# A depthwise-separable layer on one core: the first chunk of x and the third part of pw change places in the load queues

## The chip, the core and the metric

The kernel runs on one core of a Trainium2 chip. The core has a matrix engine (TensorE, PE in the profile; its weight loads are PEld), VectorE (DVE), ScalarE (ACT), GpSimd (POOL) and SyncE (SP), which here only issues transfers. Transfers between the chip's main memory (HBM) and the on-chip memory run on 16 DMA engines that all queues share. The metric is the device time of one launch in microseconds (us), the median of several runs.

## The reference

x has 384 x 384 pixels of 384 channels in bf16; dw holds one factor per channel; pw is a 384 x 384 matrix.

```python
H = W = 384
C = 384
k = 1
"x": normal(1, H, W, C) * 0.05,  "dw": normal(k, k, C) * 0.05,  "pw": normal(C, C) * 0.05

out = out + xp[:, i:i+H, j:j+W, :] * dw[i, j][None, None, None, :]   # one i, one j
return jnp.einsum('bhwc,cd->bhwd', out, pw)
```

With a 1 x 1 kernel this is one matrix product for each of 147,456 pixels: out = x · (dw ∘ pw), where row c of pw is scaled by dw[c].

## The kernel before

The factor dw is folded into pw once, at the start; after that the kernel is a stream of matrix products. Work is cut into 288 supertiles of 512 pixels. Supertiles are grouped into chunks, one load and mostly one store each: the first chunks hold 1, 1, 1, 1, 2 and 4 supertiles, the long middle 10 each, and the last ones 1 again.

**The early loads (lines 117 to 129).** `load_early` (its DMA stands at line 118 in the profile) issues five loads before anything else: dw on ScalarE's queue, three parts of pw with 128 rows each (96 KB; k = 0, 1, 2), and the first chunk of x (`X0_e`, 128 rows of 3072 bytes, 384 KB). Each load has a semaphore of its own: `s_dw`, `s_pw[0..2]`, `s_x[0][0]`. The parts k = 0 and 1 of pw and then the chunk of x are on SyncE's queue; the part k = 2 is on ScalarE's, behind dw. Each engine issues in program order. After these, SyncE goes on to its own list (`load_x`, line 170 in the profile, and `store`, line 210), sorted by due time: x's second chunk comes first. ScalarE goes on with a copy that warms it up (line 371) and then its copies below. The profile calls SyncE's queue q1 and ScalarE's q10.

**The fold (lines 278 to 314, 411 to 444).** TensorE starts with matmuls on constants that nobody reads (`idle_work`, line 134), which keep it busy until data comes. Three tiny matmuls at line 282 turn dw from a row into a column. VectorE multiplies a selection matrix by it (line 429; one call for each half of part 0, one for part 1, one for part 2). Then TensorE multiplies the selection matrix with pw, at line 306, in six units (k, r), r = 0, 1: the units of part k wait for `s_pw[k]` at line 297 as well as for VectorE's scaled selection at line 295, and part 2 also waits for the first copy out, since it writes the same PSUM banks. Unit (2, 0) runs its pair of matmuls twice. The list `w_units` (line 212) says who copies which unit from PSUM to `w_r` (line 416): VectorE the second half of unit 1 and the whole of unit 2, ScalarE the rest.

**The product (lines 252 to 275, 315 to 319).** For each supertile VectorE transposes x in 32 x 32 blocks (line 398 for the three first pieces of the first supertile, line 400 for everything else). TensorE then runs 48 matmuls at line 264, in 12 groups of four that use 32 rows of the array each and run side by side. Its first one waits for the copies of units 0 to 3 and for the first transpose; later steps of the first supertile wait for units 4 and 5. ScalarE copies each result from PSUM to the output buffer (line 469), and SyncE stores it.

The order on VectorE around the start is: scaled selections, its two copies of line 416, the transposes of the first supertile (which wait for `s_x[0][0]`), those of the second (which wait for x's second chunk). On TensorE it is: idle work, line 282, idle work, line 306 for part 0, 1 and 2, line 264.

Of the kernel before, what the change touches and what calls it, by code (L numbers as in the profile page):

```python
# [27 lines left out]
def kernel(  # L28
# [12 lines left out]
    nc = tc.nc  # L41
    P = nc.NUM_PARTITIONS
# [53 lines left out]
    s_x = [[nc.alloc_semaphore(f"s_x{i}{k}") for k in range(max(map(len, groups[i::NR])))] for i in range(NR)]  # L96
# [10 lines left out]
    s_pw = [nc.alloc_semaphore(f"s_pw{k}") for k in range(3)]  # L107
# [9 lines left out]
    def load_early(eng, dst, src, sem):  # L117
        ins = eng.dma_start(dst, src).then_inc(sem, 16)
        tc.no_tile_sem_insts.add(ins.ins.name)
        early.append(ins.ins.name)  # L120

    dw_e = dataclasses.replace(dw_h, donated_from="early_dw").ap()
    pw_e = [dataclasses.replace(raw_h, donated_from=f"early_pw{k}").ap()[:, D * k : D * k + D] for k in range(3)]
    load_early(nc.scalar, dw_e, dw.rearrange("a e c -> a (e c)"), s_dw)
    for k in range(3):
        load_early(nc.scalar if k == 2 else nc.sync, pw_e[k], pw[P * k : P * k + P, :], s_pw[k])
    x0 = xf[0:512, :].rearrange("(p s) c -> p (s c)", p=P)
    X0_e = dataclasses.replace(X0_h, donated_from="early_x0").ap()[:, 0:4].rearrange("p s c -> p (s c)")
    load_early(nc.sync, X0_e, x0, s_x[0][0])

    def idle_work(ps, n):
        for _ in range(n):
# [382 lines left out]
```

## Time and profile before

| what | us |
|---|---|
| median of 3 runs | 573.72 |
| lowest and highest run | 573.1, 574.96 |
| the profiled execution's own time | 573.13 |
| its span, first to last instruction | 571.2 |

All times within the profile count from the start of the span. A group of the profile gives a line, an engine, an operation, what it writes and reads, the count, the busy time and the mean time of one; what stands behind "idle before" is the engine's idle time ahead of the group and the event that ended most of it. A row of the timeline has start, length, engine, line and operation. A row of the DMA issues ends with the time from the issue to the last byte's landing. A row of the stretches has from:to, the length, then busy time and count of each engine, the granted clock, the DMA engines' share and GB/s.

### The profile page before, as it was taken

What the parts mean: (1) busy time and instruction counts of PE and PEld (TensorE: products, weight loads), DVE (VectorE), ACT (ScalarE), POOL (GpSimd) and SP (SyncE); (2) the same over time, 40 slices, a digit from 0 to 9 for tenths busy, and PEclk for the clock granted to TensorE, in tenths of its full rate; (3) what the DMA queues carried; (4) which work ended last, traced back from release to release, by engine and by line L of the source; (5) the groups of instructions that cost most, each with busy time, mean ns of one, the idle gap of its engine ahead of it and who ended that gap; (6) DMA issues with size and microseconds to landing.
All of it is one profiled execution on the core that took longest, in us unless ns stands there. A gap on an engine that the chain in (4) does not pass through costs nothing.

```text
span 571.2 us, 29717 instructions
## 1 busy us (share of the span) xinstructions
PE 566.9 (99%) x13841; PEld 364.2 (64%) x13841; DVE 509.3 (89%) x591; ACT 418.4 (73%) x297; POOL 13.9 (2%) x41
## 2 busy tenths in 40 slices
PE   9999999999999999999999999999999999999997
PEld 4666666666666666666666666666666666666664
DVE  7899999999999999999999999999999999999996
ACT  6777777777777777777777777777777777777775
POOL 2051000000000000000000000000000000000000
PEclk9999999999999999999999999999999999999999
DMA  8999999999999999999999999999999999997777
GB/s 323 447 385 394 432 420 428 440 421 417 425 430 430 411 379 423 411 384 392 428 399 389 413 428 400 399 410 426 399 379 425 402 392 404 417 392 317 321 286 270
DMA packets 28100, 226.88 MB, mean 397 GB/s; under 512 B 1465, under 2 KB 7866, under 8 KB 24122
## 3 DMA queue, kind: packets, MB, share of 16 engines
q1 hardware_dynamic: 27012, 225.81, 97.6%
q10 hardware_dynamic: 1078, 0.98, 0.5%
q14 instruction: 9, 0.07, 0.0%
q8 instruction: 1, 0.02, 0.0%
HBM read 113.54 MB, written 113.25 MB: 397 GB/s over the span
## 4 chain that ended last, share of the span: by engine, by line
PE 99%; ACT 0%; issue 0%
PE ps L264 98%; PE ps L306 0%; PE ps L134 0%; PE ps L341 0%; PE ps L329 0%; ACT O L464 0%; PE ps L282 0%
## 5 line engine op out<-in xcount | busy, mean ns | idle before, releaser
L264 PE MATMUL ps<-w_r,T 32*128 32x384 bf16 x13776 | 560.1, 321 | 0.0
L400 DVE STREAM_TRANSPOSE T<-X 128x384 uint32<-128x384 uint32 x571 | 500.7, 878 | 54.3 <-DMA X<-in_x_dram 1.1
L469 ACT CAST O<-ps 128x1536 bf16<-128x1536 f32 x286 | 411.7, 1440 | 146.7 <-PE ps L264 146.7
L264 PEld LDWEIGHTS ps<-w_r,T 32*128 32x128 bf16 x13776 | 361.6, 93 | 198.9 <-DVE T L398 0.7
L370 POOL COPY Xk<-Xl 32x256 bf16<-32x256 bf16 x16 | 6.3, 394 | 0.0
L369 POOL COPY Xk<-Xl 32x128 bf16<-32x128 bf16 x16 | 4.6, 288 | 25.2 <-DMA Xl<-in_x_dram 24.4
L416 ACT CAST w_r<-ps 128x768 bf16<-128x768 f32 (+1 forms) x5 | 3.4, 741 | 0.2 <-PE ps L306 0.2
L364 POOL COPY raw<-w_r 32x768 bf16<-32x768 bf16 x4 | 3.3, 820 | 5.9 <-ACT w_r L416 5.7
L134 PE MATMUL ps<-const-bfloat16-1.0 32*128 32x384 bf16 x24 | 2.2, 512 | 0.8 <-PEq L499 0.8
L371 ACT ACT_TABLE_LOAD x1 | 1.3, 1283 | 1.9 <-issue 1.9
L306 PE MATMUL ps<-raw 64*128 64x384 bf16 x14 | 2.6, 510 | 0.1
L460 DVE CAST O<-ps 128x384 bf16<-128x384 f32 x2 | 1.0, 553 | 1.4 <-PE ps L264 1.4
L306 PEld LDWEIGHTS ps<-raw 64*128 64x128 bf16 x14 | 0.8, 108 | 1.9 <-DVE raw L429 1.3
L400 DVE STREAM_TRANSPOSE T<-Xl 128x384 uint32<-128x384 uint32 x2 | 1.8, 880 | 0.2
L416 DVE CAST w_r<-ps 128x384 bf16<-128x384 f32 (+1 forms) x2 | 1.5, 758 | 0.3 <-PE ps L306 0.3
L383 DVE STREAM_TRANSPOSE T<-Xk 128x384 uint32<-128x384 uint32 x2 | 1.2, 578 | 0.5 <-PE ps L264 0.4
L341 PE MATMUL ps<-raw,T 128*128 128x384 bf16 x8 | 1.5, 327 | 0.0
L464 ACT CAST O<-ps 128x384 bf16<-128x384 f32 x2 | 1.0, 479 | 0.7 <-PE ps L341 0.7
L464 DVE CAST O<-ps 128x384 bf16<-128x384 f32 x2 | 1.1, 558 | 0.1
L459 ACT CAST O<-ps 128x384 bf16<-128x384 f32 x2 | 0.9, 482 | 0.5 <-PE ps L264 0.5
L341 PEld LDWEIGHTS ps<-raw,T 128*128 128x128 bf16 x8 | 0.7, 98 | 0.7 <-issue 0.3
L429 DVE TENSOR_SCALAR raw<-sel,ps 128x128 bf16<-128x128 f32 x2 | 0.5, 288 | 0.6 <-PE ps L282 0.6
(17 smaller groups left out, 5.0 us busy)
## 6 DMA issues: line engine op xcount, KB each, us to landing
X<-in_x_dram SPq DMA_DIRECT2D x25, 3840.0 KB, 21.8
out_dram<-O SPq DMA_DIRECT2D x25, 3840.0 KB, 27.7
X<-in_x_dram SPq DMA_DIRECT2D x3, 1536.0 KB, 18.6
X<-in_x_dram SPq DMA_DIRECT2D x2, 1920.0 KB, 14.5
out_dram<-O SPq DMA_DIRECT2D x2, 1920.0 KB, 24.0
out_dram<-O SPq DMA_DIRECT2D x2, 1536.0 KB, 13.1
X<-in_x_dram SPq DMA_DIRECT2D x6, 384.0 KB, 5.5
out_dram<-O SPq DMA_DIRECT2D x3, 768.0 KB, 5.9
```

Source lines behind the costliest of these rows:

```text
L134: mm = nc.tensor.matmul(ps[:, 2 * (i % 2) + i // 2, :D], lhsT=ones[32 * i : 32 * i + 32, 0:P], rhs=ones[32 * i : 32 * i + 32, :], start=Tr ...
L264: mm = nc.tensor.matmul(PS[s][:, q, :D], lhsT=Ts[s][32 * q : 32 * q + 32, b, par::2], rhs=w_r[32 * q : 32 * q + 32, b, par, :], start=(b, ...
L306: mm = nc.tensor.matmul(PS[(k + 1) % 2][:, 2 * r + v, :D], lhsT=sel_w[64 * v : 64 * v + 64, k, r, :, :].rearrange("p q w -> p (q w)"), rhs ...
L341: mm = nc.tensor.matmul(PS[1][:, m, :D], lhsT=Tk[:, P * (m + 2) : P * (m + 3), par], rhs=w_k[:, par, :], start=False, stop=par == 1,)
L364: nc.gpsimd.tensor_copy(w_k[quads[n]], w_r[quads[n], n]).then_inc(s_wk)
L369: nc.gpsimd.tensor_copy(Xk[quads[n], g:8:4, :], x_b).then_inc(s_xk)
L370: nc.gpsimd.tensor_copy(Xk[quads[n], 8 + g : 24 : 4, :], Xl[quads[g], :, 64 * n : 64 * n + 64]).then_inc(s_xk)
L371: nc.scalar.copy(warm[:, 0:1], nc.const_aps.tensor(0.0, [P, 1], F32)).then_inc(s_a[0])
L400: ins = nc.vector.transpose(out=Tw[:, 3 * h : 3 * h + 3], in_=Xw[:, :, j, 96 * h : 96 * h + 96].rearrange("p k (b w) -> p b k w", w=32),)
L416: o = nc.vector.tensor_copy(out, in_) if e == 0 else nc.scalar.copy(out, in_)
L464: o = (nc.scalar.copy if n % 2 else nc.vector.tensor_copy)(Ov[:, n, j, :], PS[s][:, n, :D])
L469: a = nc.scalar.copy(Ov[:, :, j, :], PS[s][:, :, :D])
```

## The change

The load of x's first chunk moves from SyncE's queue to ScalarE's, right behind dw, where the third part of pw was. The third part of pw moves to SyncE's queue, behind the other two, where x's chunk was. Sizes, destinations, semaphores and every wait stay as they are.

```diff
     load_early(nc.scalar, dw_e, dw.rearrange("a e c -> a (e c)"), s_dw)
-    for k in range(3):
-        load_early(nc.scalar if k == 2 else nc.sync, pw_e[k], pw[P * k : P * k + P, :], s_pw[k])
     x0 = xf[0:512, :].rearrange("(p s) c -> p (s c)", p=P)
     X0_e = dataclasses.replace(X0_h, donated_from="early_x0").ap()[:, 0:4].rearrange("p s c -> p (s c)")
-    load_early(nc.sync, X0_e, x0, s_x[0][0])
+    load_early(nc.scalar, X0_e, x0, s_x[0][0])
+    for k in range(3):
+        load_early(nc.sync, pw_e[k], pw[P * k : P * k + P, :], s_pw[k])
```

## The prediction

> **What bounds the kernel now.** I read the page's first line, its busy times and its chain first, to find which engine sets the end.
>
> ```profile
> span 571.2 us, 29717 instructions
> PE 566.9 (99%) x13841; PEld 364.2 (64%) x13841; DVE 509.3 (89%) x591; ACT 418.4 (73%) x297; POOL 13.9 (2%) x41
> PEclk9999999999999999999999999999999999999999
> L264 PE MATMUL ps<-w_r,T 32*128 32x384 bf16 x13776 | 560.1, 321 | 0.0
> ```
>
> TensorE is busy 99% of the span, and line 264, the product proper, holds 560.1 us of it with no idle time ahead of any of its matmuls. So nothing after the first of them can be saved or lost by a transfer, unless a new wait appears. The chain in order of time says where that stretch begins.
>
> ```profile
> 3.03 0.82 PE ps L306 x4
> 3.85 0.06 issue
> 3.91 1.78 PE ps L306 x10
> 5.69 0.02 issue
> 5.71 560.10 PE ps L264 x13772
> ```
>
> Line 264 begins at 5.71 us and runs 560.1 us. The change moves only loads of the first microseconds, so the question is whether 5.71 moves. I call that moment the start. The profiled execution took 573.13 us, 1.93 more than its span; the median of the three runs is 573.72, 0.59 more, and I carry a difference over unchanged.
>
> What holds the start at 5.71? The chain is no help: it counts TensorE as busy up to the modelled ends of its matmuls. Five queries of single DMA issues and the timeline give the landings.
>
> ```profile
> raw<-in_pw_dram SPq DMA_DIRECT2D x1, 96.0 KB, 2.1
> 1.26 0.41 SPq L118 DMA_DIRECT2D raw<-in_pw_dram  x1
> raw<-in_pw_dram SPq DMA_DIRECT2D x1, 96.0 KB, 2.5
> 1.37 0.37 ACTq L118 DMA_DIRECT2D raw<-in_pw_dram  x1
> raw<-in_pw_dram ACTq DMA_DIRECT2D x1, 96.0 KB, 2.6
> 1.72 0.43 SPq L118 DMA_DIRECT2D X<-in_x_dram  x1
> X<-in_x_dram SPq DMA_DIRECT2D x1, 384.0 KB, 3.4
> 2.36 0.33 SPq L170 DMA_DIRECT2D X<-in_x_dram  x1
> X<-in_x_dram SPq DMA_DIRECT2D x1, 384.0 KB, 4.9
> ```
>
> Issue plus time to landing: pw's second part lands at 1.26 + 2.5 = 3.8, its third at 1.37 + 2.6 = 4.0, x's first chunk at 1.72 + 3.4 = 5.1, x's second chunk at 2.36 + 4.9 = 7.3. (The first row is pw's first part.) Against these stand the consumers.
>
> ```profile
> 2.96 0.62 DVE L429 TENSOR_SCALAR raw<-sel,dw_f 128x256 bf16<-128x256 f32 x2
> 3.22 0.19 ACT L371 COPY warm<-const-float32-0.0 128x1 f32<-128x1 f32 x1
> 3.57 2.70 ACT L416 CAST w_r<-ps 128x768 bf16<-128x768 f32 x4 [0.15 <-PE ps L306]
> 3.88 0.16 PEld L306 LDWEIGHTS ps<-raw 64*128 64x128 bf16 x4 [0.62 <-DVE raw L429]
> 4.45 0.96 DVE L416 CAST w_r<-ps 128x768 bf16<-128x768 f32 x1
> 4.48 0.20 PEld L306 LDWEIGHTS ps<-raw 64*128 64x128 bf16 x4 [0.44 <-issue]
> 5.32 0.69 DVE L398 STREAM_TRANSPOSE T<-X 128x128 uint32<-128x128 uint32 x3
> 5.68 0.45 PEld L264 LDWEIGHTS ps<-w_r,T 32*128 32x128 bf16 x9 [0.69 <-DVE T L398]
> ...
> L416 ACT CAST w_r<-ps x5: 484/799/817, 3.6 to 6.2; 128x768 bf16<-128x768 f32 x4, 128x384 bf16<-128x384 f32 x1
> ```
>
> The fold of pw's second part starts at 3.88 after 0.62 us of idle. The view names VectorE's line 429, but that pair ended at 2.96 + 0.62 = 3.58, so it was not the last to come: it was the landing at 3.8, on which the same line of code waits. From there the path is tight: that fold, VectorE's second copy (4.45, 0.96 long, so to 5.41), its first transpose (5.32, overlapping), the first weights of line 264 at 5.68. **pw's second part sets the start.** Its third is not late: it lands at 4.0, its fold starts at 4.48, and ScalarE's first copy of 0.8 us (the last row's median; 3.57 to 4.37) is what that fold waits for too. x's first chunk is not late either: it lands at 5.1, and VectorE is in its copy until 5.41.
>
> **The change, part by part.** *x's first chunk goes to ScalarE's queue, issued second.* It is issued at about 1.37 instead of 1.72, 0.35 earlier. That removes no wait, since VectorE's copy hides the landing. Were the copy not there, the gain would end at the 0.35. ScalarE itself issues for 0.43 instead of 0.37 us, which pushes its table load and the warm copy (3.22, 0.19 long) by 0.06; the 0.15 us of idle before its first cast at 3.57 covers that.
>
> *pw's third part goes to SyncE's queue, third.* It is issued at 1.72 instead of 1.37, and it now stands behind the first two on one queue. SyncE still issues three loads before its own stream, so x's second chunk is still issued near 2.36, behind 96 KB instead of 384 KB on its queue, but with the same bytes ahead of it in all. I cost this at nothing: today it comes at 7.3 with no idle on line 264, and a later start only gives it room.
>
> *What shares the DMA engines with pw's second part changes.* That is the part that costs. Two stretches of the DMA view, 1.8 to 2.6 and 2.6 to 3.5 us, and two more, 3.0 to 3.5 and 3.5 to 4.3:
>
> ```profile
> q1 hardware_dynamic: 201, 0.14, 67.9%
> ...
> q1 hardware_dynamic: 106, 0.11, 69.6%
> q10 hardware_dynamic: 144, 0.10, 34.2%
> ...
> DMA packets 98, 0.10 MB, mean 206 GB/s; under 512 B 18, under 2 KB 80, under 8 KB 98
> q1 hardware_dynamic: 37, 0.07, 87.4%
> q10 hardware_dynamic: 61, 0.04, 22.7%
> ...
> q1 hardware_dynamic: 82, 0.25, 85.2%
> ```
>
> q1 is SyncE's queue, q10 ScalarE's. Up to 2.6 q1 moved 0.14 MB, pw's first part (0.1 MB) and somewhat under half of the second; q10's load, issued at 1.37, began only after 2.6. Its 144 packets took 34.2% of 16 engines for 0.9 us, so 0.034 us each: pw's third part is light company. Put x's first chunk in that place and the company is heavy. From 3.5 to 4.3 its 82 packets took 85.2% of 16 x 0.8 us, 0.133 us each. Earlier they are worse: from 3.0 to 3.5 the 18 packets over 2 KB (98 less 80) hold nearly all of q1's 87.4% of 16 x 0.5 us, 7.0 us; less 15 or so small ones at 0.034 that is about 0.36 us each. These are the first packets of x, and there is one per engine.
>
> So at 2.6 each of the 16 engines has some four small packets of pw's second part to go, and x's packets come between them. If the two queues take turns, an engine spends 0.36 + 3 x 0.133 = 0.76 us more on x in that time, where it now spends 4 x 0.034 = 0.14 on pw's third part. That is +0.6 for an engine that has them all still to do; but a landing counts the slowest engine, and the slowest now is not the one that will meet the worst x packet. Bounds: at best pw's second part loses its rival and lands like the first, in 2.1 instead of 2.5 us, 0.4 earlier, of which 0.25 reaches the start: the third fold still waits for ScalarE's first copy, begins at 4.48 and has three pairs of matmuls to run, about 0.32 us each at the rate found below, to 5.45. At worst it lands when x's chunk would, 3.4 us after ScalarE's issue: 1.37 + 3.4 = 4.8, 1.0 later. I take **+0.5 us**, near the packet count.
>
> pw's third part then comes last. It queues behind the second, and all four loads together land by 5.1 today, so that is its bound. I put it at 4.9. Its fold would start at 5.0; with the second fold 0.5 later it starts at 4.48 + 0.5 = 5.0 anyway. Both paths give a start of 5.71 + 0.5 = 6.2.
>
> Sum: first chunk earlier 0, issue on ScalarE 0, second part of pw +0.5, third part hidden behind that. 573.13 + 0.5 = 573.6 against the profiled execution, **574.2** against the median.
>
> **A price that could be less than its size: TensorE's rate.** PEclk says 9 everywhere, yet the spacing says otherwise.
>
> ```profile
> 0.84:2.10 1.26, 1.26 (x16) 0.51 (x16) 1.00 0.16 38
> 5.71:6.24 0.53, 0.53 (x8) 0.32 (x12) 1.00 0.95 383
> 8.00:568.00 560.00, 557.81 (x13732) 360.13 (x13728) 1.00 0.99 401
> ```
>
> 16 warm-up matmuls of line 134 took 1.26 us, 0.315 for four that run side by side; the first 8 of line 264 took 0.53, 0.265 for four; later four take 557.81 x 4 / 13732 = 0.162. So TensorE runs at half rate up to about 6.2, and work done before that costs double. Here a start that moves from 5.7 to 6.2 leaves no slow product: 0.2 of the 0.5 comes back, and in a run where the rate rises later than the start, half does. I keep the whole 0.5, because the same delay is idle time for TensorE, which speaks for the first rival.
>
> **The rivals.** *The full rate comes later (slower than before).* TensorE is fed nearly without a break from 0.84, and full rate came after 5.4 us. With pw's second and third parts late, the 0.62 us of idle at 3.88 grows to about 1.1. If the rate depends on how busy TensorE was, it can miss its turn. Every microsecond of product at half rate costs 0.5. A whole further 5.4 us would cost 2.7; the runs of before spread from 573.1 to 574.96, 1.9, which a varying turn would explain, and I take that: 574.2 + 1.5 for a turn missed in most but not all runs, 575.7. It decides once the added idle is more than the rate control forgives. For it: the spread, and that the first 2 us of dense matmuls were not enough. Against it: a 0.62 us gap was forgiven in this execution. The Trainium skill, "TensorE: Matmul & The Clock Gate", Part 1 (The HAM clock gate), says that the clock is halved until a free-running window of about 3.4 us was busy; by it a missed window would cost 1.7 us, an estimate from that page. The half rate up to 6.2 agrees with it; how busy a window must be, no row here shows.
>
> *x goes as a block.* If an engine, once on ScalarE's queue, finishes its share of x before it turns back, pw's second part meets its worst bound, +1.0: 574.7. For it: at 384 KB over 16 engines the share is only eight rows, 0.36 + 7 x 0.133 = 1.3 us. Against it: q1 and q10 both moved packets from 2.6 to 3.5. The Trainium skill, "DMA: Bandwidth & Descriptors", section "Queues, rings and completion order", says that an engine changes queues only between packets of some 9 to 17 descriptors; that would be this case, and the rows above, in which both queues are served, do not decide it.
>
> *Nothing is lost.* x's first packets meet engines that are done with pw's second part, which lands as now or up to 0.4 earlier: 573.5. For it: a good part of that load was through by 2.6, and on SyncE's queue pw's parts no longer share with one another. Against it: every byte of x that moves before 3.8 is new competition there. That the edit does not do what it says would end here as well.
>
> **How the numbers follow.** Forecast 574.2 with 0.40; rate later, 575.7, 0.28; x as a block, 574.7, 0.17; nothing lost, 573.5, 0.15. A measurement of this kernel can tell about 0.3%, 1.7 us, from no change: slower means over 575.4, faster under 572.0. Of the rate's 0.28 some 0.22 lies over 575.4, and I add 0.02 for a rate missed on top of a block: slower 0.24. Faster would need more than the 0.25 that the best bound gives: 0.02. The rest, 0.74, is within. The range runs from 573.2, below the "nothing lost" case, to 576.0, above the rate's, and leaves out about 0.15; the likeliest case alone has 573.7 to 574.8.
>
> **What would show it.** Right: the fold of pw's second part starts at 4.2 to 4.6 instead of 3.88, its third near 5, line 264 at 6.0 to 6.5, and line 264 keeps 560 us. Rate later: line 264's busy time rises towards 562, with matmuls of 0.5 us long after 6.2. Block: the second fold at 4.9. Nothing lost: 3.5 to 3.9. I would be wrong altogether if line 264 showed idle time later on, which would mean that x's second chunk or the stream behind it slipped.

## The result and the profile after

The changed kernel takes 575.2 us (median of 10 runs, 573.54 to 578.03); the kernel before took 573.4 in the same comparison (10 runs, 573.02 to 574.96). The ratio is 1.0032 with a 95% interval of 1.0018 to 1.0045: a small slowdown, which the interval separates from no change. The prediction counted as slower what lies over 575.4; 575.2 lies just under that. The profiled execution took 575.4 us, 2.27 more than the one of before.

First the page of the changed kernel, the lines that answer to those shown of before, and its chain in order of time (start, length, what):

```profile
span 573.4 us, 29717 instructions
PE 567.9 (99%) x13841; PEld 384.8 (67%) x13841; DVE 510.4 (89%) x591; ACT 418.1 (73%) x297; POOL 13.9 (2%) x41
L264 PE MATMUL ps<-w_r,T 32*128 32x384 bf16 x13776 | 561.1, 322 | 0.0
```

```profile
1.26 3.79 DMA raw<-in_pw_dram
5.05 0.14 issue
5.18 1.78 PE ps L306 x10
6.97 0.02 issue
6.99 561.10 PE ps L264 x13449
```

Line 264 still has no idle time ahead of its matmuls. What changed is its two ends: it starts at 6.99 instead of 5.71, 1.28 later, and is busy 561.1 instead of 560.1 us, 1.0 more. Together that is the whole 2.27. Now the view itself names pw's second part as what TensorE waited for: issued at 1.26, it landed 3.8 us later, at 5.05, where it had landed at 3.8.

The landings of the other two, again from queries of single issues (last column: us from issue to landing):

```profile
X<-in_x_dram ACTq DMA_DIRECT2D x1, 384.0 KB, 4.0
raw<-in_pw_dram SPq DMA_DIRECT2D x1, 96.0 KB, 3.9
```

The first row is x's first chunk, the second pw's third part. The chunk, issued 0.35 earlier, lands at 1.37 + 4.0 = 5.4, later than the 5.1 of before. pw's third part lands at 1.72 + 3.9 = 5.6 instead of 4.0. None of the three gained. The stretch of 2.6 to 3.4 us shows why; the last two numbers are the DMA engines' share and GB/s, first of before, then of the changed kernel:

```profile
2.60:3.40 0.80, 0.78 (x12) 0.26 (x4) 0.76 (x5) 0.79 (x2) 0.00 (x0) 1.00 1.10 247
```

```profile
2.60:3.40 0.80, 0.75 (x12) 0.26 (x4) 0.76 (x5) 0.79 (x2) 0.00 (x0) 1.00 0.17 24
```

For 0.8 us the engines moved a tenth of what they moved before, with loads issued on both queues. They were not busy with x; by this view they were mostly idle (share 0.17). The two later profiles of the changed order have the same hole, less deep: 50 GB/s in `after_again` and 52 in `after_fed`.

The other half is TensorE's rate. Line 264 in three stretches of the changed kernel (from:to, length, then busy time and count of its matmuls and of its weight loads, the granted clock, the DMA engines' share and GB/s):

```profile
6.99:9.50 2.51, 2.51 (x32) 1.40 (x36) 1.00 1.06 430
9.72:11.68 1.96, 1.96 (x56) 1.33 (x49) 1.00 1.02 429
11.68:568.00 556.32, 556.32 (x13699) 379.11 (x13688) 1.00 0.99 399
```

The first 32 matmuls took 2.51 us, 0.31 for four side by side; the later 13699 took 0.162 for four. The half rate, which ended at about 6.2 before, now lasted to about 9.6. As before, the granted clock in these rows reads 1.00 throughout; in the views only the spacing tells. The trace's own record of the clock has its first entry where full rate begins, at 6.18 us in the profile of before and at 9.62 here, and the views show 1.00 where there is no entry. Full rate then lasts 566.61 us before and 563.20 here, 3.41 less.

### The profile page after: what moved, and what is told of

Same layout as the page of the kernel before. It is cut to its first block, busy times and chain, and to the rows that moved or that the text cites. A ratio compares the mean times of both kernels' runs of the same rounds, so it can differ in the third digit from the quotient of the medians.

```text
span 573.4 us, 29717 instructions
## 1 busy us (share of the span) xinstructions
PE 567.9 (99%) x13841; PEld 384.8 (67%) x13841; DVE 510.4 (89%) x591; ACT 418.1 (73%) x297; POOL 13.9 (2%) x41
## 3 DMA queue, kind: packets, MB, share of 16 engines
q10 hardware_dynamic: 1078, 1.28, 0.6%
## 4 chain that ended last, share of the span: by engine, by line
PE 99%; DMA 1%; ACT 0%; SPq 0%; issue 0%
PE ps L264 98%; DMA raw<-in_pw_dram 1%; PE ps L306 0%; PE ps L341 0%; PE ps L329 0%; ACT O L464 0%; SPq L118 0%
## 5 line engine op out<-in xcount | busy, mean ns | idle before, releaser
L264 PE MATMUL ps<-w_r,T 32*128 32x384 bf16 x13776 | 561.1, 322 | 0.0
L264 PEld LDWEIGHTS ps<-w_r,T 32*128 32x128 bf16 x13776 | 382.0, 93 | 179.4 <-DVE T L398 0.7
```

Source lines behind the costliest of these rows:

```text
L264: mm = nc.tensor.matmul(PS[s][:, q, :D], lhsT=Ts[s][32 * q : 32 * q + 32, b, par::2], rhs=w_r[32 * q : 32 * q + 32, b, par, :], start=(b, ...
```

## The experiments

There are twelve runs. Each is compared with the kernel before on the same chip. For every profile but three, time is start of line 264 + its busy time + 7.3 us (7.30 to 7.32, with the chain's figures), so a run is read from two numbers. The three exceptions, 7.6 to 7.7, are among the four with extra matmuls. In some of the edited kernels the product stands at line 265 or 268. The diffs show what the text is about; where x's chunk comes in several loads, the number that its wait counts to is raised to match. Each run has one profile, so a landing here is that of one execution.

### Is it x's queue, or x's company?

```diff
+    for k in range(3):
+        load_early(nc.scalar if k == 2 else nc.sync, pw_e[k], pw[P * k : P * k + P, :], s_pw[k])
     load_early(nc.scalar, X0_e, x0, s_x[0][0])
-    for k in range(3):
-        load_early(nc.sync, pw_e[k], pw[P * k : P * k + P, :], s_pw[k])
```

> x's first chunk stays on ScalarE's queue but is issued third there, behind pw's third part, about 1.8 us; SyncE has only pw's first two parts ahead of its stream. Theory 'company' (what costs is that x is under way while pw's second part is): pw's second part lands near 3.8 as before the change, line 264 starts at 5.7 to 5.9, time within 0.1% of before. Rival 'queue' (x on ScalarE's queue costs wherever it stands, since the two queues are served in turn): the second part lands at 4.5 or later, start 6.4 or later, time 1 us or more over before.

Ratio 1.0053 (1.0037 to 1.0069). The landing of pw's second part is as "company" has it, in 2.4 us, at 3.7. The start is not: 7.10. Another wait took the place, and it is not pw's. First single DMA issues, then the chain, then a row of the timeline, of this run:

```profile
raw<-in_pw_dram SPq DMA_DIRECT2D x1, 96.0 KB, 2.4
...
X<-in_x_dram ACTq DMA_DIRECT2D x1, 384.0 KB, 4.9
```

```profile
1.77 0.44 ACTq L118
...
2.40 1.28 ACT L371
...
3.89 3.21 ACT w_r L416 x5
7.10 561.11 PE ps L264 x12054
```

```profile
6.73 0.70 DVE L398 STREAM_TRANSPOSE T<-X 128x128 uint32<-128x128 uint32 x3 [1.43 <-DMA X<-in_x_dram]
```

The chain names ScalarE's copies, but it only names what ended last by the profile. The first matmul of line 264 waits for three of these five copies, those of units 0, 1 and 3, and the third of them ended at 4.85 + 0.81 = 5.66 by the timeline. What it waited for is x's chunk: it lands at 1.77 + 4.9 = 6.7, VectorE idles 1.43 us for it, and the start follows the landing by 0.39 us, as it does in the next run. ScalarE's third issue does put off its table load, from 1.93 to 2.40, but the copies behind that do not reach the start. So the queue as such does not delay pw; x's chunk, issued 0.4 us later than in the changed kernel, is late itself.

### The half with pw alone

```diff
-    load_early(nc.scalar, X0_e, x0, s_x[0][0])
     for k in range(3):
         load_early(nc.sync, pw_e[k], pw[P * k : P * k + P, :], s_pw[k])
+    load_early(nc.sync, X0_e, x0, s_x[0][0])
```

> The half of the change that moves pw's third part to SyncE's queue, without the other half: x's first chunk stays on SyncE's queue, now fourth; ScalarE's queue has dw alone. Theory 'company': pw's second part has nothing beside it, lands at 3.4 to 3.8; the third follows at 3.8 to 4.2; start 5.5 to 5.8; time as before or up to 0.3 us less. Rival 'third part': if the third part's place behind the second is what delays the start, line 264 starts at 6.2 or later.

Ratio 1.0004 (0.9992 to 1.0016): no difference that can be told. With only dw on the other queue, pw's second part lands in 2.0 us, at 3.3, the third at 1.72 + 2.2 = 3.9. The start is 6.39 all the same, which I had not expected: x's chunk, issued at 2.19, lands at 6.0 and now sets it. The issue of the second part, then the chain:

```profile
raw<-in_pw_dram SPq DMA_DIRECT2D x1, 96.0 KB, 2.0
```

```profile
2.19 3.81 DMA X<-in_x_dram
6.00 0.02 issue
6.02 0.32 DVE T L398
6.34 0.05 issue
6.39 559.83 PE ps L264 x13776
```

Part of the later start is made up by the rate: 559.83 us busy means full rate from the first matmul, 0.27 us less than before, against a start 0.68 later. That pw's third part stands third on SyncE's queue does not make it late: it landed at 3.9, as in the profile of before.

### Which packets of x: a quarter, four quarters, three quarters, or pw's own rows

A quarter of each row on ScalarE's queue, the rest behind pw:

```diff
-    load_early(nc.scalar, X0_e, x0, s_x[0][0])
+    load_early(nc.scalar, X0_e[:, 0:C], x0[:, 0:C], s_x[0][0])
     for k in range(3):
         load_early(nc.sync, pw_e[k], pw[P * k : P * k + P, :], s_pw[k])
+    load_early(nc.sync, X0_e[:, C:], x0[:, C:], s_x[0][0])
```

> As the changed kernel, but only the first of the four 768-byte pieces of each of the 128 rows of x's first chunk is loaded on ScalarE's queue (96 KB, the size that pw's third part has); the other three pieces follow on SyncE's queue behind pw's third part. All of the chunk is loaded, in two transfers. Theory 'bytes' (x's large packets take turns with pw's): with packets of pw's own size the second part of pw lands at 3.7 to 4.0, start 5.6 to 5.9, time as before. Rival 'first reads' (the first reads of x hold up the engines, whatever their size): it lands at 4.6 or later, start 6.5 or later.

pw's second part landed in 2.1 us, at 3.3, earlier than either theory had it: first reads of x in rows of 768 bytes beside it do no harm. Start 6.72, set by the remaining three quarters that land at 6.3 (a miss: I had not thought of them); ratio 1.0016 (1.0001 to 1.0030).

All of the chunk in pieces of pw's size, on the same queue:

```diff
-    load_early(nc.scalar, X0_e, x0, s_x[0][0])
+    for j in range(4):
+        load_early(nc.scalar, X0_e[:, C * j : C * j + C], x0[:, C * j : C * j + C], s_x[0][0])
```

> The changed kernel with x's first chunk in four loads of 96 KB (128 rows of 768 bytes each) one behind the other on ScalarE's queue instead of one load of 128 rows of 3072 bytes: same queue, same bytes, small packets, issued over 1.4 to 3 us. Theory 'packet size' (a packet of pw waits for a four times longer packet of x at each turn, and for its slow first ones): the second part of pw lands at 3.3 to 3.9, the third at 4.3 to 5.0. Rival 'same bytes, same wait': the second part at 4.0 or later and the third at 5.4 or later, as in the changed kernel. Start 6.2 to 7.0, since x's last piece is issued later or pw's third part lands late.

The issue of the second part, and the chain:

```profile
raw<-in_pw_dram SPq DMA_DIRECT2D x1, 96.0 KB, 2.3
```

```profile
2.73 6.42 DMA X<-in_x_dram
...
9.54 561.26 PE ps L265 x13114
```

Second part in 2.3 us, at 3.6; third at 1.72 + 2.8 = 4.5: as "packet size" has it. The time is 1.0075 (1.0051 to 1.0099, four runs) of before, because the fourth piece lands 6.4 us after its issue and the start moves to 9.54, far beyond my 7.0. The test of packet size is not clean: four issues also spread the bytes over time.

pw's rows in x's place, read into an output buffer that is still free, with x's chunk behind pw on SyncE's queue:

```diff
-    load_early(nc.scalar, X0_e, x0, s_x[0][0])
+    load_early(nc.scalar, Z_e, pw.rearrange("(p s) c -> p (s c)", p=P), s_z)
     for k in range(3):
         load_early(nc.sync, pw_e[k], pw[P * k : P * k + P, :], s_pw[k])
+    load_early(nc.sync, X0_e, x0, s_x[0][0])
```

> In the place on ScalarE's queue that x's first chunk has in the changed kernel stands an extra load that nothing reads: all of pw in 128 rows of 2304 bytes (288 KB) into an output buffer not yet in use. x's first chunk is fourth on SyncE's queue, as in the run with everything on SyncE's queue, whose second part of pw landed at 3.3. Theory 'bytes': large rows from any tensor beside pw's parts delay them; the second part lands at 4.0 or later and the third at 5.0 or later. Rival 'x' (it is x's rows in main memory that answer slowly): the second part lands at 3.3 to 3.7, the third at 3.9 to 4.4. Either way x's chunk lands late (6.0 or more) and sets the start, so the time is over before.

```profile
raw<-in_pw_dram SPq DMA_DIRECT2D x1, 96.0 KB, 3.3
```

Second part in 3.3 us, at 4.6, third at 5.0, against 3.3 and 3.9 without the extra load: large rows of another tensor than x delay it too. Ratio 1.0035 (1.0019 to 1.0051), start 7.32 by x's chunk.

The same size of row and the same bytes, from x:

```diff
-    load_early(nc.scalar, X0_e, x0, s_x[0][0])
+    load_early(nc.scalar, X0_e[:, 0 : 3 * C], x0[:, 0 : 3 * C], s_x[0][0])
     for k in range(3):
         load_early(nc.sync, pw_e[k], pw[P * k : P * k + P, :], s_pw[k])
+    load_early(nc.sync, X0_e[:, 3 * C :], x0[:, 3 * C :], s_x[0][0])
```

> As the changed kernel, but on ScalarE's queue stand three of the four 768-byte pieces of each row of x's first chunk as one piece of 2304 bytes (288 KB), and the fourth follows on SyncE's queue behind pw's third part. It has the packet size and the bytes of the run that put pw's own rows there; only the source differs. In that run the DMA engines moved 190 GB/s from 2.6 to 3.4 us and pw's second part landed at 4.6; in the changed kernel they moved 24. Theory 'bytes': as with pw's rows, 150 to 250 GB/s, second part at 4.2 to 4.8. Rival 'x': under 80 GB/s in that stretch, as in the changed kernel, second part at 4.1 to 5.1.

Second part at 4.93, a little later than "bytes" allowed and within what "x" allowed; the rate in the stretch, 130 GB/s, lies between the two. Neither theory is borne out. Ratio 1.0036 (1.0023 to 1.0048, five runs). The stretch of 2.6 to 3.4 us side by side, for a quarter of x, pw's rows, and three quarters of x:

```profile
2.60:3.40 0.80, 0.80 (x12) 0.26 (x4) 0.77 (x5) 0.79 (x2) 0.00 (x0) 1.00 0.92 266
```

```profile
2.60:3.40 0.80, 0.80 (x13) 0.18 (x10) 0.69 (x4) 0.79 (x2) 0.00 (x0) 1.00 0.77 190
```

```profile
2.60:3.40 0.80, 0.80 (x13) 0.18 (x10) 0.67 (x4) 0.79 (x2) 0.00 (x0) 1.00 0.55 130
```

With rows of 768 bytes beside pw's the engines moved 266 GB/s (258 for the whole chunk in four pieces), with rows of 2304 bytes 190 from pw and 130 from x, with x's whole rows 24 to 52: the larger the rows beside pw's parts, the deeper the hole, and deeper for x than for pw. pw's third part follows the same order: it landed at 4.3 to 4.6, 5.0, 5.3 and 5.6 to 5.8. That large rows beside pw's delay it is shown.

What the engines wait for in the hole, and how much of it is x's own, stays open. One rival was not separated: the slow time may belong to the first large rows that a run moves, wherever they stand. With everything on SyncE's queue, x's first rows came at 3.3, queued behind all of pw, and the engines moved 166 GB/s from 3.4 to 4.2; in the quarter run they moved 141 there, when the first rows over 2 KB began, where the changed kernel, past its hole, moved 374. In those two runs pw's second part had already landed.

### The changed kernel again

> The changed kernel itself, unedited, for a second profile and a comparison on the same chip as the others of this call. Its profile had the second part of pw at 5.05, the fed version 4.1, both the third part at 5.6. If the third part's landing sets the start, a second profile has it at 5.4 to 5.8 and line 264 at 6.8 to 7.1 whatever the second part does between 4.1 and 5.1; if the second part sets it, the start follows that part by 1.9 us. Time 575.0 to 575.6.

Median 575.22; on this chip the kernel before was spread wider, with a median of 574.13, so the ratio is 1.0013 (0.9997 to 1.0030): here the change can't be told from none. The second profile is worth more than the ratio, since it shows the late start without the late rate. From its chain:

```profile
1.26 3.55 DMA raw<-in_pw_dram
4.81 0.14 issue
4.95 0.50 PE ps L306 x4
5.45 0.40 issue
5.85 0.66 PE ps L306 x6
6.51 0.04 issue
6.55 559.83 PE ps L264 x13776
```

The second part lands at 4.81, the third at 5.7 to 5.8, the start is 6.55, below what I gave for the third part as its cause. The second part alone accounts for the start, through VectorE's copy and first transpose; the start follows its landing by 1.7 us, less than the 1.9 at half rate. But the third part is no longer hidden: TensorE stands idle for 0.40 us until it lands, and its fold ends at 6.51 as well. Here the two paths end together. Full rate came ahead of line 264: 559.83 us busy, and this execution took 573.69 us, 0.56 over that of before. So the same kernel ran in 573.69 with full rate early and in 575.4 with full rate late.

### Is the rate a matter of TensorE's idle time?

The changed kernel with TensorE kept busy during its wait:

```diff
         for k in range(3):
+            if k == 1:
+                idle_work(PS[0], 4)
             for r in range(2):
```

> The changed kernel with 16 more idle matmuls of line 134's kind (four times four) between the fold of pw's first part and that of its second, on PSUM banks that nothing reads. At half rate they take about 1.3 us, as long as the wait for pw's second part. Theory 'idle' (the full rate came one step later because TensorE stood idle from 3.7 to 5.1): line 264 still starts near 7.0, but at full rate or at most half a microsecond from it; its busy time falls from 561.1 back to 560 or less; time 0.7 to 1.2 us under the changed kernel's, about 574.2. Rival 'turn' (the rate's turn has nothing to do with that idle time): no difference from the changed kernel, or later by what the matmuls take too long.

```profile
raw<-in_pw_dram SPq DMA_DIRECT2D x1, 96.0 KB, 2.8
...
6.91 559.83 PE ps L264 x13776
```

The first row is the issue of pw's second part, the last is from the chain. Start as in the changed kernel, busy time 1.3 less: full rate was there in time. Median 574.61, 0.6 under the changed kernel's, ratio 1.0022 (1.0012 to 1.0033). The gain is a little less than I gave; five of ten runs still lie over 574.6, a line that here tells little, since the profiled execution, with full rate early, itself took 574.43. In this profile pw's second part landed in 2.8 us, at 4.1, a microsecond earlier than in the first, and it was the added matmuls that held its fold until 5.1; the third part landed at 5.6 as before.

The kernel before with less to do for TensorE:

```diff
-                for v in [0, 1] * (2 if (k, r) == (2, 0) else 1):
+                for v in [0, 1]:
```

> The kernel before without the repeated pair of matmuls in unit (2, 0) of the fold (its result is the same without it): TensorE stands idle 0.3 us more around 5 us, while the start of line 264 at 5.7, which hangs on the copies, should not move. Theory 'idle': more runs have the full rate one turn later, near 574.9; the median rises by 0.3 to 1.7 us. Rival 'turn': the turn is chance alone, median within 0.2 us of before.

Median 574.02, ratio 1.0013 (1.0002 to 1.0025). Six of 12 runs lie over 574.6, of before on that chip 4 of 30, and none lies between 573.41 and 574.64. The profile is one of the early ones:

```profile
1.72 3.93 DMA X<-in_x_dram
...
6.04 559.83 PE ps L264 x13776
```

It shows something that I had not expected, since the start was not to move: with pw's second part at 3.6, x's chunk at 5.65 set the start, 0.33 later than in the first profile of before.

And with more to do, a filler of four idle matmuls between the first two parts of the fold, tried twice, and once with unit (2, 1) doubled too:

```diff
+            if k == 1:
+                idle_work(PS[0], 1)
...
-                for v in [0, 1] * (2 if (k, r) == (2, 0) else 1):
+                for v in [0, 1] * (2 if k == 2 else 1):
```

> The kernel before with 4 idle matmuls (0.3 us at half rate) between the fold of pw's first part and that of its second, where TensorE stands idle for some 0.3 us. Theory 'idle' (idle time between the folds decides in which turn the full rate comes): the runs near 574.9, where I take the turn to have been missed, become rarer and the median falls by 0 to 0.3 us. Rival 'turn': the same spread as before, the median the same or up to 0.2 us longer.

> The kernel before with the 4 idle matmuls, a second time. If the first result holds (one of 12 runs over 574.6, against 14 of 29 of before on the same chip), at most a quarter of the runs lie over 574.6, and the median is 573.4 to 573.9; the low runs are 0.2 to 0.4 us over the low runs of before, since a landing in time now finds TensorE occupied.

> The kernel before with the 4 idle matmuls between the fold's first two parts and with unit (2, 1)'s pair of matmuls run twice as well, so that TensorE is also busy from 5.5 to the start. Theory 'idle': hardly any run near 574.9; median 573.2 to 573.8. Rival 'turn': a third of the runs or more near 574.9, as before on the same chip.

In the order shown, 1 of 12, 0 of 12 and 1 of 12 runs lie over 574.6; of before on the same chips it was 13 of 29 for the first (not 14, as the second expectation has it) and 4 of 30 for the others. The medians are 573.65, 573.41 and 573.45, the ratios 0.9991 (0.9978 to 1.0003), 1.0002 (0.9993 to 1.0011) and 1.0006 (0.9994 to 1.0017). On the first chip feeding TensorE removed most of the late runs; on the other, where the kernel before had few, 1 of 24 against 4 of 30 shows little. Its own cost is that the early runs take 0.3 to 0.4 us longer (lowest 573.23 against 572.85 and 573.04 against 572.75). None of them is shown to beat the kernel before.

The traces' records of the clock show why one kernel has early and late runs. In all 14 profiles full rate lasts either 566.61 or 563.20 us, and it begins at 3.85 to 6.56 us in the eight with the longer time, at 9.62 to 12.50 in the six with the shorter. That is what steps of 3.41 us give, if full rate can begin only at a step and the steps lie differently in each execution. Count back one step from full rate. In the profile of before the stretch from 2.77 to 6.18 had TensorE busy for 3.31 of 3.41 us. In the first profile of the changed kernel the stretch from 2.79 to 6.20 held the wait for pw's second part, TensorE was busy for 2.06 of it, and full rate came one step later, at 9.62. In the second profile the step came at 3.95, before that wait, after 3.03 us busy, and full rate with it. How much idle time is too much can't be read from these profiles: stretches after which full rate came had 2.65 us busy and more, those that were passed over 2.82 and less.

## Why the prediction was right or wrong

*What bounds it: right.* Only the first 10 us changed, line 264 has no new idle time, and in both profiles of the changed kernel pw's second part accounts for the start, as the prediction read from its landing against the name that the view gave.

*x's chunk earlier is worth nothing: right, and less than that.* It landed later, 5.4. But "not late either" was read from one profile. In that of the starved kernel the same load, in the same place, landed at 5.65 and set the start; in the first fed one it landed at 5.87 and did too. The margin is a few tenths, and it differs between executions.

*pw's third part hidden behind the second: right in the first profile, barely in the second, and wrong in its bound.* It landed at 5.6 and 5.7 to 5.8, not 4.9, and past the 5.1 within which all four loads landed before. The bound took the bytes per time for fixed. The hole in the stretch of 2.6 to 3.4 us left 0.18 MB unmoved (0.8 us x 223 GB/s).

*"I take +0.5 us, near the packet count": the step that failed.* The mechanism, large rows beside pw's second part, is borne out by the quarter, by pw's rows and by the pw half alone, with one profile each. The same loads land differently from one execution to the next: the second part at 3.6 to 4.2 in the five profiles with the order of before, at 4.1 to 5.05 in the three with the changed order; the third part is clear of that, 3.9 to 4.4 against 5.6 to 5.8. In the two profiles of the changed kernel itself the second part landed 1.0 and 1.3 us later than in that of before, and the start moved by 0.84 and 1.28 instead of 0.5; one of the two lies above the worst bound of 1.0. The count gave each engine its share of packets at their own length; it had no term for engines that stand idle.

*The rate: the first rival, at 0.28, is what mostly happened.* In the first profile line 264 took 1.0 us more; 16 of the changed kernel's 20 runs lie over 574.6, of the 98 runs of before in all these comparisons 23 did. Its chance was too low, and its time of 575.7 too high by half a microsecond. The first hint was in the spread of before, 573.1 to 574.96, which the prediction read so but gave little weight. That idle time moves the turn is seen from both sides, with less work (6 of 12 late against 4 of 30) and with more (1 of 12 against 13 of 29), in small counts, and in the traces' records of the clock. The Trainium skill, "TensorE: Matmul & The Clock Gate", Part 1, gives a free-running window of about 3.4 us. The steps of 3.41 us, and their different places in the 14 profiles, agree. The prediction's estimate of 1.7 us for a missed window was not paid in full: line 264's busy time was 1.0 and 1.3 us longer than in the profiles of before and of the second look, because the late start had moved out of part of that window. How much idle time a window forgives no run here measured.

*x as a block:* it forecast the second fold at 4.9, and 4.95 and 5.18 were seen, but for another reason: in the hole hardly a packet moved on either queue, 14 on SyncE's and 3 on ScalarE's from 2.6 to 3.4 us in the first profile.

*Nothing is lost:* wrong in the changed kernel, whose second and third parts of pw both landed later.

The range of 573.2 to 576.0 held 575.2, but by the width that the first rival gave it and not by the sum: the likeliest value of 574.2 did not come about, since the start came 1.28 and 0.84 us later instead of 0.5, and in most runs the late rate came on top.

## What to carry to other kernels

Two loads on two queues are not independent: judge the place of a large load by what lands later on the other queue, not by its own issue time. Putting it behind the small ones on which the first compute waits frees those, but only as far as the large one is not needed soon itself: with everything on SyncE's queue it set the start in their place, and nothing was gained. Where TensorE's rate rises only after steady work, a wait in the prologue can cost about as much again through the rate as by its length (1.0 beside 1.28 us here), and it shows as two groups of run times rather than as a shift; look at the spread before pricing a wait. A landing that is "not late" by a few tenths in one profile can be late in the next.

## What the runs showed of the hardware

- Loads of 128 rows of 3072 bytes on one queue and 128 of 768 on the other left the 16 DMA engines nearly idle for 0.8 us (24 GB/s, share 0.17; 50 and 52 GB/s in two further profiles); with 768-byte rows on both they moved 266 GB/s in the same stretch.
- TensorE ran at half rate until 6.18 us in one profile and 9.62 in another, and in others full rate was there before the product began, while the granted clock in the profile's rows read 1.00. Over 14 profiles full rate lasted 566.61 or 563.20 us, 3.41 apart.
- One more load issued by ScalarE, 0.44 us of its time, moved its table load from 1.93 to 2.40 us.
